# One M2 tile in 64-row halves between the score bursts of a quad, in an attention and MLP kernel on one core

## The chip, the cores and the metric

The kernel runs on one core of a Trainium2 chip. The time is the device time of one execution in microseconds (us); the figure given for a kernel is the median of its runs. A profiled execution gives, beside that, the span from its first to its last instruction. TensorE is called PE in the profile, its weight loads PEld, VectorE is DVE, ScalarE is ACT, GpSimd is POOL, SyncE is SP.

## What is computed

Causal attention with a decay made of a cumulative sum, for 8 batches of 8 heads, 576 positions and 64 values a head; then a two-layer MLP with SiLU over the 4608 tokens. The reference, cut to this:

```python
# q, k, v: (8, 8, 576, 64); f: (8, 8, 576); w_in: (512, 2048); w_out: (2048, 512), all float32
scores = q @ k.transpose(0, 1, 3, 2) / sqrt(64)
cum = cumsum(log(clip(f, 1e-4, 1.0)), axis=-1)
scores = where(causal, -1e9, scores + cum[..., :, None] - cum[..., None, :])
attn = softmax(scores, axis=-1)
x = (attn @ v).transpose(0, 2, 1, 3).reshape(4608, 512)
h = x @ w_in
out = (h * sigmoid(h)) @ w_out
```

## The kernel before

**Units and quads.** Two heads of one batch make a unit n (32 of them); two units, n and n+1, make a quad m = 0 to 15. The first 128 positions of every head are done ahead of the quads, in a first part of the kernel; each quad does the other 448 positions of its four heads.

**Attention of a unit.** scores(n, c) makes the transposed scores in three bursts c = 0, 1, 2 (L444 to L472). A head has 64 values, so its matmuls contract over 64 rows; the two heads of a unit lie in the two halves of the array's rows, and each pair of matmuls (i = 0, 1) writes to two PSUM banks. A burst takes one tile `sc` of two banks from the pool psc, which has two such tiles, and ScalarE reads it with exp into `u` (c = 0, 1 and part of 2) and `ut` (the last 64 positions, L467). mask(n) (L474) and mask_tail(n) (L480) set the entries above the diagonal to zero on VectorE. attend(n) (L490) multiplies with the values: 18 matmuls of 128x65 from `u` (L506) and 10 from `ut` (L515) into a tile `dn` of pbig, of which the fifth of each five on `ut` reads the part that mask_tail writes; then VectorE takes the reciprocal of the sums (L523) and divides (L524).

**Loads.** turn(n) casts unit n+2 on POOL and transposes it by a DMA on the SP queue (L427) into one of three tiles `qkT`; prepare(n) issues the loads of unit n+4 on SP and converts values on POOL; back(m) brings a quad's result into the MLP's layout, from quad 3 to 14 by two DMA transposes on SP (L538, L542; the list BY_DMA).

**The MLP.** The tokens form 13 groups of 512, 256 or 384 columns (GW): group 0 to 2 hold the first 128 positions, the others the rest of one batch each, or the last 64 positions of four batches. M1 makes a group's hidden layer in 16 chunks: m1_chunk(g, fc) runs four matmuls over all 128 rows into a tile `hp` of pbig (L567), ScalarE computes tanh of half of it (L575), VectorE makes the activation in `gt` (L576). `gt` has two buffers. M2 makes 128 tokens' output: m2_part(g, tb, part) runs 4 of the 16 matmuls of 128x512 (L612) into a tile `po` of pbig; after the fourth part ScalarE copies it with a factor 0.5 into `osb` (L622), and a DMA on the POOL queue stores it. `po` of one tile, `hp`, `dn` and other tiles share the four banks of pbig, in turn.

**The order.** Every engine's order is the program's. Attention and MLP are woven by hand: between the pieces of a quad stand slots, slot(us), that call fill(us). fill plans M1 chunks and M2 parts for as long as its budget is above zero, at fixed prices of 0.863 us an M2 part and 0.650 us an M1 chunk of 384 columns (0.437 for 256); what it overdraws is kept in at["left"] and comes off the next slot. wanted() chooses M1 or M2 so that M2 of the group before proceeds evenly with M1 of a group (L641 to L654). M1 of a group may not begin while M2 is more than one group behind. A slot then issues the stores that were recorded before it, and counts down the groups that wait to become ready.

Of the kernel before, what the change touches and what calls it, by code (L numbers as in the profile page):

```python
# [18 lines left out]
def kernel(  # L19
# [540 lines left out]
    def m1_chunk(g, fc):  # L560
        w = GW[g]
        if fc == 0:
            gts[g] = gpool.tile([P, NFC, w], BF16, name="gt", tag="gt")
        gt = gts[g]
        hp = pbig.tile([P, w], FP32, name="hp", tag="big")
        for cc in range(NCC):
            nc.tensor.matmul(  # L567
                hp[:, :],
                lhsT=w_in_bf[:, cc, fc * P : (fc + 1) * P],
                rhs=xcols(g, cc),  # L570
                start=(cc == 0),
                stop=(cc == NCC - 1),
            )
        th = tpool.tile([P, w], BF16, name="th", tag="th")
        nc.scalar.activation(out=th[:, :], in_=hp[:, :], func=ACT.Tanh, scale=0.5)  # L575
        nc.vector.scalar_tensor_tensor(  # L576
            out=gt[:, fc, :],
            in0=th[:, :],
            scalar=1.0,
            in1=hp[:, :],  # L580
            op0=ALU.add,
            op1=ALU.mult,
        )
# [4 lines left out]
    def store(n):  # L588
        n = max(n, 0)
        for q_, dst, src in stores[:n]:  # L590
            q_.dma_start(out=dst, in_=src)  # L591
        del stores[:n]
# [33 lines left out]
                stores.append((q_, out[t0 : t0 + r.stop - r.start, m0:m1], osb[r, :]))  # L626


    M1 = [(g, fc) for g in range(NG) for fc in range(NFC)]
    M2 = []  # L630
    for g in range(NG):
# [3 lines left out]
    at = {"m1": 0, "m2": 0, "left": 0.0}  # L635
    ready: set[int] = set()
    open2 = {"w": False}

    begin: dict[int, tuple[int, int]] = {}

    def wanted(a, c):  # L641


        g1 = M1[a][0] if a < len(M1) else NG
        g2 = M2[c][0] if c < len(M2) else NG
        can1 = g1 in ready and not (M1[a][1] == 0 and g1 > g2 + 1)
        can2 = open2["w"] and c < len(M2) and g2 < g1
        if not can1 or not can2:
            return 1 if can1 else 2 if can2 else 0
        a0, c0 = begin.get(g1, (M1[a][1], c)) if M1[a][1] else (0, c)  # L650
        c1 = sum(M2_OF[:g1])
        f1 = (M1[a][1] - a0 + 0.5) / (NFC - a0)
        f2 = (c - c0 + 0.5) / max(1, c1 - c0)
        return 1 if f1 <= f2 else 2  # L654

    def step(force=0):

        a, c = at["m1"], at["m2"]
        want = wanted(a, c)
        if not want:  # L660
            return None
        g1 = M1[a][0] if a < len(M1) else NG
        g2 = M2[c][0] if c < len(M2) else NG
        can1 = g1 in ready and not (M1[a][1] == 0 and g1 > g2 + 1)
        can2 = open2["w"] and c < len(M2) and g2 < g1
        kind = force if (force == 1 and can1) or (force == 2 and can2) else want
        if kind == 1:
            if M1[a][1] == 0:
                begin[g1] = (0, c)
            m1_chunk(g1, M1[a][1])  # L670
            at["m1"] += 1
            t = 4 * (GW[g1] / 2.4 + 2.5)
        else:
            m2_part(*M2[c])
            at["m2"] += 1
            t = 4 * (DM / 2.4 + 2.5)
        return t

    def behind():
        t = sum(4 * (GW[g] / 2.4 + 2.5) for g, _ in M1[at["m1"] :] if g in ready)  # L680
        t += sum(4 * (DM / 2.4 + 2.5) for g, _, _ in M2[at["m2"] :] if g in ready)
        return t / 1000
# [49 lines left out]
    scores0(0, bans[0])  # L732
    weights()
    setup_pool.__exit__(None, None, None)
    gpool = ctx.enter_context(tc.tile_pool(name="gpool", bufs=2))
    convert_v0(0)
    load_w_in(0)
    turn0(1, 0)
# [100 lines left out]
    def turn(n):  # L839
        if 0 < n < NU - 2:  # L840
            cast_qk(n + 2)
            transposes(n + 2)

    def prepare(n):
# [13 lines left out]
        if p >= 2:  # L858
            for c in range(2 * (p - 2), 2 * (p - 1)) if b > 0 else range(NM * (p - 2)):
                convert_v(b + 1, c)  # L860

    LAG = 13.0
    pending: list = []

    def slot(us_, *ends):
        n = len(stores)
        fill(us_, 0, ends)
        store(n)
        for x in pending:
            x[0] -= 1  # L870
        while pending and pending[0][0] == 0:
            ready.update(pending.pop(0)[1])

    for m in range(NQ):
        n = 2 * m
        piece = 1.7 if m < 2 else 2.4
        scores(n, 0)
        scores(n, 1)
        turn(n)
        if m > 0:  # L880
            back(m - 1)
            if m % 2 == 0:
                b = m // 2 - 1
                pending.append([2, [REST_OF[b]] + ([TAILS_OF[b][0]] if b == NM - 1 else [])])
        prepare(n)
        slot(piece, 1, 0)
        mask(n)
        scores(n, 2)
        scores(n + 1, 0)
        turn(n + 1)  # L890
        prepare(n + 1)
        slot(piece, 1, 0)
        mask_tail(n)
        mask(n + 1)
        scores(n + 1, 1)
        scores(n + 1, 2)
        mask_tail(n + 1)
        slot(piece, 1, 0)
        attend(n)
        attend(n + 1)  # L900
        slot(min(3.5, max(0.8, behind() - LAG)) if m > 1 else 0.8)
    back(NQ - 1)
    ready.update([REST_OF[B - 1], TAILS_OF[B - 1][0]])
    for x in pending:
# [35 lines left out]
```

## Time and profile before

| what | value | where from |
|---|---|---|
| time, median of 3 runs | 343.55 us | runs (343.11 to 345.07) |
| span of the profiled execution | 342.2 us | page |
| median less that span | 1.35 us | difference |
| M2 matmuls of 128x512 (L612) | 560 | groups by shape |
| score matmuls on 64 rows (L459) | 768 | groups by shape |
| evictions of 128x512 (L622) | 35, mean 609 ns | groups by shape |
| quad 7, first score to first score of quad 8 | 150.36 to 164.91 us | TensorE's timeline |

The profile is of one execution; its span lies a little under the times of the runs, which also hold what is ahead of the first and behind the last instruction. A matmul's duration in it is modelled, since matmuls are pipelined: two starts tell more than a duration. The 13 groups' M1 and M2 and the 16 quads fill the span to about 280 us; behind that stand only M1 and M2.

### The profile page before, as it was taken

Reading aid. Unit: us, or ns where it says so; the run is one execution under the profiler, and the core shown is the slowest. Engines: PE = TensorE matmul, PEld = TensorE weight load, DVE = VectorE, ACT = ScalarE, POOL = GpSimd, SP = SyncE. Lnnn points to the kernel's source line nnn. Section 1 sums busy time; section 2 is a strip of 40 time slices with the busy share of each in tenths; the row PEclk is TensorE's granted clock in tenths of the full one; section 3 lists DMA queues with packets and bytes.
Section 4 is the critical chain, followed back from the end, with each engine's and each line's share of the span. In section 5 each row is a group of like instructions: output and inputs, shape, how many; then the busy total and the mean of one; then the engine's idle time right before and its main releaser. Section 6 shows DMA issues by size and latency. Waiting matters only on the chain.

```text
span 342.2 us, 8881 instructions
## 1 busy us (share of the span) xinstructions
PE 334.3 (98%) x3560; PEld 198.6 (58%) x3560; DVE 180.5 (53%) x387; ACT 216.8 (63%) x401; POOL 130.0 (38%) x227
## 2 busy tenths in 40 slices
PE   7999999999999999999999999999999999999995
PEld 3645655567656556566465666656656565555654
DVE  4665736357647547357445563655746364444330
ACT  5857645877687676857759677595685944454431
POOL 8895317732618307327325422612830000001011
PEclk9999999999999999999999999999999999999999
DMA  8999999999699889999999789989994010001012
GB/s 154 185 184 221 192 192 155 233 207 190 142 172 205 188 177 168 180 210 156 174 188 188 171 156 202 169 170 165 165 186 101 22 42 33 31 32 61 33 53 72
DMA packets 142457, 50.67 MB, mean 148 GB/s; under 512 B 133328, under 2 KB 139728, under 8 KB 142416
## 3 DMA queue, kind: packets, MB, share of 16 engines
q1 hardware_dynamic: 132400, 32.93, 56.7%
q0 software_dynamic: 9856, 17.04, 21.5%
q8 instruction: 28, 0.46, 0.6%
q10 hardware_dynamic: 160, 0.13, 0.1%
q14 instruction: 13, 0.11, 0.1%
HBM read 36.85 MB, written 9.44 MB: 135 GB/s over the span
## 4 chain that ended last, share of the span: by engine, by line
PE 66%; DMA 14%; SPq 9%; POOL 6%; issue 3%; ACT 0%; POOLq 0%
PE po L612 29%; PE hp L567 25%; DMA vf<-in_v_dram 6%; PE sc L459 5%; SPq L158 5%; PE dn L506 4%; DMA w_out_bf<-in_moe_w_out_dram 3%; PE dn L515 2%; SPq L427 2%; DMA qkT<-qkb 2%; POOL qkb L399 1%; DMA qkb<-in_k_dram 1%; SPq L168 1%; SPq L179 1%; DMA qf<-in_q_dram 1%
## 5 line engine op out<-in xcount | busy, mean ns | idle before, releaser
L576 DVE SCALAR_TENSOR_TENSOR gt<-th,hp 128x384 bf16<-128x384 bf16 (+2 forms) x208 | 105.8, 522 | 119.0 <-ACT th L575 115.5
L575 ACT ACTIVATE th<-hp 128x384 bf16<-128x384 f32 (+2 forms) x208 | 95.2, 478 | 84.3 <-PE hp L567 82.0
L612 PE MATMUL po<-w_out_bf,gt 128*128 128x512 bf16 (+1 forms) x592 | 145.3, 374 | 0.0
L567 PE MATMUL hp<-x,w_in_bf 128*128 128x384 bf16 (+2 forms) x704 | 128.1, 321 | 0.2
L567 PEld LDWEIGHTS <-w_in_bf 128*128 128x128 bf16 x832 | 79.9, 98 | 56.5 <-issue 0.7
L463 ACT ACTIVATE u<-sc 128x1024 bf16<-128x1024 f32 (+1 forms) x96 | 75.3, 822 | 9.5 <-PE sc L459 9.5
L612 PEld LDWEIGHTS <-gt 128*128 128x128 bf16 x592 | 53.3, 98 | 47.9 <-issue 2.5
L591 POOL DMA_DIRECT2D out_dram<-osb x38 | 21.0, 552 | 93.7 <-ACT osb L622 66.7
L413 POOL TENSOR_TENSOR vp<-vf,w_bf 128x520 bf16<-128x520 f32 (+1 forms) x32 | 34.4, 1078 | 41.0 <-DMA vf<-in_v_dram 35.1
L622 ACT ACTIVATE osb<-po 128x512 f32<-128x512 f32 (+1 forms) x37 | 22.1, 597 | 18.9 <-PE po L612 18.9
L399 POOL CAST qkb<-qf 128x384 bf16<-128x384 f32 x32 | 16.7, 521 | 41.9 <-DMA qf<-in_q_dram 41.2
L459 PE MATMUL sc<-qkT 64*128 64x128 bf16 (+1 forms) x640 | 26.9, 207 | 0.9 <-DMA qkT<-qkb 0.8
L459 PEld LDWEIGHTS <-qkT 64*128 64x128 bf16 x640 | 18.4, 94 | 12.5 <-issue 10.2
L467 ACT ACTIVATE ut<-sc 128x640 bf16<-128x640 f32 x32 | 23.3, 729 | 0.0
L476 DVE TENSOR_TENSOR u<-u,tri 128x768 bf16<-128x768 bf16 x32 | 22.1, 690 | 1.2 <-ACT u L463 1.2
L399 POOL CAST qkb<-kf 128x384 bf16<-128x384 f32 x32 | 17.7, 554 | 13.0 <-DMA kf<-in_k_dram 12.8
L506 PEld LDWEIGHTS <-u 128*128 128x128 bf16 x576 | 20.8, 98 | 2.5
L506 PE MATMUL dn<-vp,u 128*128 128x65 bf16 x384 | 21.8, 194 | 0.0
L524 DVE TENSOR_TENSOR xr<-dn,rec 128x448 bf16<-128x448 f32 x32 | 20.0, 624 | 1.1
L506 PE MATMUL dn<-v,u 128*128 128x65 bf16 x192 | 19.8, 194 | 0.0
L482 DVE TENSOR_TENSOR ut<-ut,trit 128x128 bf16<-128x128 bf16 x32 | 11.2, 351 | 15.6 <-ACT ut L467 15.6
L567 PE MATMUL hp<-xt,w_in_bf 128*128 128x256 bf16 x128 | 17.7, 273 | 0.0
(68 smaller groups left out, 203.0 us busy)
## 6 DMA issues: line engine op xcount, KB each, us to landing
out_dram<-osb POOLq DMA_DIRECT2D x32, 256.0 KB, 3.3
vf<-in_v_dram SPq DMA_DIRECT2D x26, 256.0 KB, 4.7
qf<-in_q_dram SPq DMA_DIRECT2D x64, 96.0 KB, 2.9
kf<-in_k_dram SPq DMA_DIRECT2D x64, 96.0 KB, 3.1
w_in_bf<-in_moe_w_in_dram POOLq DMA_DIRECT2D x4, 512.0 KB, 6.9
w_out_bf<-in_moe_w_out_dram POOLq DMA_DIRECT2D x4, 512.0 KB, 9.6
vf<-in_v_dram POOLq DMA_DIRECT2D x6, 256.0 KB, 10.3
qkb<-in_q_dram POOLq DMA_DIRECT2D x8, 128.0 KB, 5.1
```

The costliest lines, as they stand in the source:

```text
L399: nc.gpsimd.tensor_copy(out=t2[:, c0 : c0 + NR, :].rearrange("p c x -> p (c x)"), in_=t[:, :, :, :].rearrange("p c h d -> p (c h d)"),)
L413: nc.gpsimd.tensor_tensor(out=vbf[b][r, c, :, :], in0=vst[b][c][r, :, :], in1=w_bf[r, c + 1, b * H : (b + 1) * H, None].to_broadcast([n, H ...
L459: nc.tensor.matmul(sc[:, i, o : o + q1 - q0], lhsT=kt, rhs=t[r, q0:q1], start=True, stop=True)
L463: nc.scalar.activation(out=u[:, :, c * SM : c * SM + w], in_=sc[:, :, 0:w], func=ACT.Exp, scale=scale)
L467: nc.scalar.activation(out=ut[:, :, 0:3:2, :].rearrange("p k i t -> p i k t"), in_=sc[:, :, T0 : T0 + (NM + 1) * ST].rearrange("p i (k t) ...
L476: nc.vector.tensor_tensor(out=x, in0=x, in1=tri[:, None, None, :].to_broadcast([P, 2, NR, P]), op=ALU.mult)
L506: nc.tensor.matmul(dn[:, i * NR + c - 1, :], lhsT=u[:, i, o : o + P], rhs=vals(kb, i), start=(kb == 0), stop=(kb == c),)
L567: nc.tensor.matmul(hp[:, :], lhsT=w_in_bf[:, cc, fc * P : (fc + 1) * P], rhs=xcols(g, cc), start=(cc == 0), stop=(cc == NCC - 1),)
L575: nc.scalar.activation(out=th[:, :], in_=hp[:, :], func=ACT.Tanh, scale=0.5)
L576: nc.vector.scalar_tensor_tensor(out=gt[:, fc, :], in0=th[:, :], scalar=1.0, in1=hp[:, :], op0=ALU.add, op1=ALU.mult,)
L612: nc.tensor.matmul(po[:, :], lhsT=gt[:, fc, tb * P : (tb + 1) * P], rhs=w_out_bf[:, fc, m0:m1], start=(fc == 0), stop=(fc == NFC - 1),)
L622: nc.scalar.activation(out=osb[:, :], in_=po[:, :], func=ACT.Copy, scale=0.5)
```

## The change

From m = 4 on, a quad asks whole() for an M2 tile whose group M1 has finished. whole() first runs the rest of a tile that is partly done, and charges those parts to the budget; if there is no whole tile of an earlier group, the quad runs as before. With a tile, the quad's order is another: the three slots between the bursts are gone. m2_rows(g, tb, half) stands between the first and second and between the second and third pair of bursts. It contracts 64 rows at a time: for each of 8 of the 16 fc, two matmuls, rows 0 to 63 into one tile of pbig and rows 64 to 127 into another. m2_join then adds the two tiles on VectorE in two operations, with the factor 0.5, into `osb`. After the bursts come attend(n), mask_tail(n+1), a slot of 1.3, attend(n+1), a slot of 2.4 and the last slot as before. The row tile itself is not charged to the budget.

The planner changes as well: M2 may be two groups behind from m = 2 on, and from m = 4 M2 runs in the slots only when more than 12 parts of groups ahead of M1's are left; behind the loop this is taken back. `gt` therefore has three buffers, in three tags; the first of them gives its memory to another pool after group 0.

```diff
@@ m1_chunk @@
-            gts[g] = gpool.tile([P, NFC, w], BF16, name="gt", tag="gt")
+            gts[g] = gpools[g % 3].tile([P, NFC, w], BF16, name="gt", tag=f"gt{g % 3}")
@@ after m2_part @@
+    def m2_rows(g, tb, half):
+        gt = gts[g]
+        if half == 0:
+            pos[g, tb] = [pbig.tile([P, DM], FP32, name="pr", tag="big") for _ in range(2)]
+        for fc in range(half * NFC // 2, (half + 1) * NFC // 2):
+            for z, po in enumerate(pos[g, tb]):
+                r = slice(z * D, (z + 1) * D)
+                nc.tensor.matmul(
+                    po[:, :],
+                    lhsT=gt[r, fc, tb * P : (tb + 1) * P],
+                    rhs=w_out_bf[r, fc, :],
+                    start=(fc == 0),
+                    stop=(fc == NFC - 1),
+                )
+
+    def m2_join(g, tb):
+        lo, hi = pos[g, tb]
+        store(len(stores) - 3)
+        osb = opool.tile([P, DM], FP32, name="osb", tag="osb")
+        nc.vector.tensor_scalar(
+            out=osb[:, :], in0=lo[:, :], scalar1=0.5, scalar2=None, op0=ALU.mult
+        )
+        nc.vector.scalar_tensor_tensor(
+            out=osb[:, :], in0=hi[:, :], scalar=0.5, in1=osb[:, :], op0=ALU.mult, op1=ALU.add
+        )
+        for r, b, s0 in rows_of(g, tb):
+            t0 = b * S + s0
+            stores.append((nc.gpsimd, out[t0 : t0 + r.stop - r.start, :], osb[r, :]))
@@ the planner @@
+    lag = {"g": 1, "parts": 0}
...
-        can1 = g1 in ready and not (M1[a][1] == 0 and g1 > g2 + 1)
+        can1 = g1 in ready and not (M1[a][1] == 0 and g1 > g2 + lag["g"])
         can2 = open2["w"] and c < len(M2) and g2 < g1
+        if can1 and can2 and lag["parts"]:
+            return 2 if sum(M2_OF[:g1]) - c > lag["parts"] else 1
@@ ahead of the quads @@
-    gpool = ctx.enter_context(tc.tile_pool(name="gpool", bufs=2))
+    gpool = ctx.enter_context(tc.tile_pool(name="gpool", bufs=1))
+    first_pool = tc.tile_pool(name="first", bufs=1)
+    gpools = [first_pool.__enter__(), gpool, gpool]
...
+    def whole():
+
+        while at["m2"] < len(M2) and M2[at["m2"]][2] and wanted(at["m1"], at["m2"]):
+            t = step(2)
+            at["left"] -= t / 1000
+        a, c = at["m1"], at["m2"]
+        if c >= len(M2) or M2[c][2]:
+            return None
+        g1 = M1[a][0] if a < len(M1) else NG
+        return M2[c][:2] if M2[c][0] < g1 else None
+
...
+    def passed():
+        for x in pending:
+            x[0] -= 1
+        while pending and pending[0][0] == 0:
+            ready.update(pending.pop(0)[1])
@@ the loop over the quads @@
+        if m == 2:
+            assert at["m2"] >= M2_OF[0]
+            first_pool.__exit__(None, None, None)
+            gpools[0] = ctx.enter_context(tc.tile_pool(name="third", bufs=1))
+            lag["g"] = 2
+        if m == 4:
+            lag["parts"] = 12
+        rows = whole() if m > 0 and BY_DMA[m - 1] else None
         scores(n, 0)
         scores(n, 1)
         turn(n)
...
         prepare(n)
+        if rows:
+            at["m2"] += 4
+            m2_rows(*rows, 0)
+            mask(n)
+            scores(n, 2)
+            scores(n + 1, 0)
+            turn(n + 1)
+            prepare(n + 1)
+            m2_rows(*rows, 1)
+            mask_tail(n)
+            mask(n + 1)
+            scores(n + 1, 1)
+            scores(n + 1, 2)
+            m2_join(*rows)
+            passed()
+            attend(n)
+            mask_tail(n + 1)
+            slot(1.3)
+            attend(n + 1)
+            slot(2.4)
+            slot(min(3.5, max(0.8, behind() - LAG)))
+            continue
         slot(piece, 1, 0)
...
+    lag["parts"] = 0
     back(NQ - 1)
```

More of the change, by code (lines that the diff above doesn't have):

```diff
@@ L663, in step @@
         g2 = M2[c][0] if c < len(M2) else NG
-        can1 = g1 in ready and not (M1[a][1] == 0 and g1 > g2 + 1)
+        can1 = g1 in ready and not (M1[a][1] == 0 and g1 > g2 + lag["g"])
         can2 = open2["w"] and c < len(M2) and g2 < g1
@@ L868, in slot @@
         store(n)
[L869 to L872, printed above, removed]
+        passed()
     for m in range(NQ):
@@ L885 @@
         prepare(n)
+        if rows:
[12 more added lines that the diff above has]
+            m2_join(*rows)
+            passed()
+            attend(n)
[5 more added lines that the diff above has]
+            continue
         slot(piece, 1, 0)
```

## The prediction

> **What bounds the kernel.** I read the page first, then TensorE's timeline over one quad in the middle (quad 7 of 0 to 15, 150.36 to 164.91 us), then those of ScalarE and VectorE beside it, then the groups by shape. All times are us unless marked ns.
>
> ```profile
> span 342.2 us, 8881 instructions
> PE 334.3 (98%) x3560; PEld 198.6 (58%) x3560; DVE 180.5 (53%) x387; ACT 216.8 (63%) x401; POOL 130.0 (38%) x227
> PEclk9999999999999999999999999999999999999999
> ```
>
> TensorE is busy 98% of the span at full clock; no other engine passes 63%. In quads 5 to 15 I compared each matmul's start with its predecessor's plus its streaming time: apart from one wait of 0.11, nothing but changes of the array's mode adds time. So what is taken off TensorE's stream comes off the end, and any new wait of TensorE is added in full.
>
> ```profile
> 149.77 0.65 PE L567 MATMUL hp<-x,w_in_bf 128*128 128x384 bf16 x3
> 150.36 0.40 PE L459 MATMUL sc<-qkT 64*128 64x128 bf16 x8
> 150.59 0.33 PE L459 MATMUL sc<-qkT,kT 64*128 64x384 bf16 x2
> 150.75 0.22 PE L459 MATMUL sc<-qkT 64*128 64x128 bf16 x2
> 150.91 1.04 PE L612 MATMUL po<-w_out_bf,gt 128*128 128x512 bf16 x4
> 151.78 2.11 PE L567 MATMUL hp<-x,w_in_bf 128*128 128x384 bf16 x12
> ```
>
> The first column is the start, the durations are modelled, so I use starts. M1 matmuls of 384 columns follow each other every 0.1625 (151.78 on). The last of the first three starts at 150.10 and the scores at 150.36 instead of 150.26: 0.10 to enter the 64-row mode. The last pair of scores, at 150.75, takes 0.056 like the four pairs before it (0.23 for eight matmuls); M2 could start at 150.81 and starts at 150.91: another 0.10 to leave. Over all switches of the trace the first step is 0.096 and 0.092 too long and the step after it 0.008 and 0.010: **0.206 for a round trip**. The pair of 64x384 ends 0.16 after it starts (150.59 to 150.75), which is one matmul's time: two 64-row halves in different rows of the array and different PSUM banks run together.
>
> **What the change takes off.** The planner's counters, followed through the new code by its own prices (0.863 for an M2 part, 0.650 for an M1 chunk of 384), put the row path into quads 5 to 15, 11 quads; in quad 4 M2 has no tile of an earlier group. Each had three round trips and keeps one: 22 x 0.206 = **-4.5**. The tile itself is 16 pairs of 64x512 for 16 matmuls of 128x512, which start every 0.216. From the 64x384 row a pair costs the same; were the halves serial, 11 x 16 x 0.216 = +38. I take the row, with up to 0.008 a pair (+1.4) for the range. The page "TensorE: Matmul & The Clock Gate" of the Trainium skill, section "Measured speedup vs the span model", reports 3.07 instead of 4 for four row tiles at 512 columns; by that share an estimate is 0.28 a pair and +11 in all, which the 64x384 pair speaks against.
>
> **What it adds: a wait of scores(n+1,0).** psc has two buffers, so scores(n+1,0) waits for the exp of scores(n,1). Two row halves of 8 x 0.216 = 1.73 now stand where slots of 2.4 stood.
>
> ```profile
> 150.85 1.94 ACT L463 ACTIVATE u<-sc 128x1024 bf16<-128x1024 f32 x2
> 251.07 0.60 ACT L622 ACTIVATE osb<-po 128x512 f32<-128x512 f32 x1 [0.37 <-PE po L612]
> 251.56 1.94 ACT L463 ACTIVATE u<-sc 128x1024 bf16<-128x1024 f32 x2
> 62.43 1.02 ACT L463 ACTIVATE u<-sc 128x1024 bf16<-128x1024 f32 x1
> 63.50 0.40 PE L459 MATMUL sc<-qkT 64*128 64x128 bf16 x8
> ```
>
> From a quad's first score on, the two exps end at 2.43 where an M1 chunk's tanh stands before them (150.36 to 152.79) and at 2.54 where an eviction does (quad 14, 250.96 to 253.50). Quad 0 shows this very wait: exp ends at 63.45, the scores start at 63.50, 0.05 later. TensorE now arrives at 0.45 + 1.73 + 0.21 (scores(n,2)) = 2.39: it waits 0.05 to 0.10 in six quads and 0.20 in the five (6, 8, 10, 13, 15) where whole() has just finished a tile whose eviction stands before the exps. Sum **+1.55**. Behind it on TensorE stand the second row half and the third burst, all of which move by the wait; ScalarE then gets exp(n+1,0) from 2.59 on but is busy with exp(n,2) until 3.43, so it loses nothing. The third burst does not wait: exp(n+1,0) ends at 4.47, its buffer is wanted at 4.77.
>
> **What it adds: a wait of attend(n+1).** M2 parts that whole() runs are charged to the budget, so slot(1.3) can come out empty. Quad 5 ends with a budget of -0.07 and one part of tile (3,2) done; whole() runs three (-2.66), and 1.3 more is still below zero. The same happens in quads 8, 10 and 13 (three, two and one part). There attend(n+1) follows attend(n) directly, and its matmuls on the tail need mask_tail(n+1), which on VectorE stands behind mask(n+1), the join and attend(n)'s division.
>
> ```profile
> L476 DVE TENSOR_TENSOR u<-u,tri 128x768 bf16<-128x768 bf16 x32 | 22.1, 690 | 1.2 <-ACT u L463 1.2
> L292 DVE CAST kT<-tp 128x512 bf16<-128x512 f32 x8 | 5.5, 689 | 4.5 <-PE tp L285 4.5
> L523 DVE RECIPROCAL rec<-dn 128x7 f32<-128x7 f32 x32 | 6.4, 199 | 2.2 <-PE dn L515 2.2
> L524 DVE TENSOR_TENSOR xr<-dn,rec 128x448 bf16<-128x448 f32 x32 | 20.0, 624 | 1.1
> L482 DVE TENSOR_TENSOR ut<-ut,trit 128x128 bf16<-128x128 bf16 x32 | 11.2, 351 | 15.6 <-ACT ut L467 15.6
> L236 DVE TENSOR_SCALAR f_sb<-f_sb 64x576 f32<-64x576 f32 x1 | 0.5, 452 | 0.0
> ```
>
> The join's two operations on 512 floats from PSUM are not in the trace. The cast from PSUM at 689 ns is nearest (same shape, same source); L236 at 452 (SBUF only) bounds it below, and above I add the 0.13 by which mask_tail's mean, 351, exceeds its undisturbed 0.22: 0.45 to 0.82, I take 0.69. From the quad's first score: mask(n+1) 4.50 to 5.19, first half 5.10 to 5.80 (an independent operation starts 0.08 before the last one ends: two L576 of 0.55 take 1.02), second half 5.84 to 6.53, reciprocal 6.44 to 6.64, division to 7.30, mask_tail to 7.57. TensorE is free at 5.91 and would end attend(n+1) at 6.75; the last six matmuls of 0.03 wait until 7.62 and end at 7.80: 1.05, or 0.79 with the masks at 0.55 and 0.22. I take 0.9, four times: **+3.6**. Behind it on TensorE stands slot(2.4), for which no other engine is waiting. With a join of 0.45 it is 0.4 each, with 0.82 it is 1.3. Where the slot holds two M1 chunks (1.30), attend(n+1) reaches the mask at 7.87 and waits for nothing. Quad 15 (one chunk) pays some 0.25, quad 11 (three chunks of 256, so dn(n+1) takes dn(n)'s buffer) some 0.15: **+0.4**.
>
> The page "TensorEngine Tiling (Array Packing)", section "PSUM Bottleneck", advises evicting with both ScalarE and VectorE when row tiles fill PSUM faster; the change puts both halves on VectorE. With one half on ScalarE, which stands idle there, by that rule the wait would be about 0.3 and the sum near -1.4.
>
> **What it moves, at no cost.** The eviction (L622, 0.61) leaves ScalarE in 11 tiles; ScalarE was off the path. The M1 chunks gather in the last slots: one every 0.65 on TensorE, 0.42 on ScalarE and 0.47 on VectorE, and from a chunk's first matmul to its buffer free is 2.0, under the 2.6 that four buffers give; with one buffer fewer (1.95) each chunk of a long row would wait 0.05. No DMA is added; stores stay on POOL, now behind both casts of the quad; the row tile's store waits there for the join (6.53), ahead of the next quad's casts, which stood behind an eviction at 8.3 in quad 8 before. scores(n+1,0) comes 0.3 to 1.2 earlier in its quad, so its DMA-transposed qkT is wanted earlier. SP issues nearly without a gap, and qkT(17) lands at 166.72 for 167.94, 1.2 ahead; most odd units have 2 to 2.8. Where the slack is least (quad 6, 0.5; quad 8, 1.2) whole()'s parts push the scores back by 2.6, so I price it at nothing. The looser M2 order costs nothing: same matmuls, and the code behind the loop ends with the same tile.
>
> **Sum.** -4.5 + 1.55 + 3.6 + 0.4 = **+1.0**. Against the profiled 342.2 the span becomes 343.2; the median of the runs lies 1.35 above that span, so 343.55 becomes **344.5**. The first measured digit that can be told from no change I put at 0.5%, 1.7.
>
> **Rivals.** (a) *The waits stay short*: the tail's masks are ready in time, say because VectorE evicts 512 floats at L236's rate or the four empty slots get work. For it: the waits are differences of chains several us long. Against it: the VectorE order is fixed by the program. It leaves -4.5 + 1.55 = -3.0: 340.6. (b) *VectorE becomes the bound of the row quads*, the slower side: the join is dearer than 0.82. From 0.25 later on at mask_tail(n+1) the five quads with two chunks wait as well. At 1.0 an operation the four pay 1.5, the five 0.4: -4.5 + 1.55 + 6.0 + 2.0 + 0.4 = +5.4: 349. For it: mask_tail's mean is 1.6 times its undisturbed time, so VectorE is disturbed there. Against it: 53% busy. (c) *qkT lands late*, because the SP queue does not follow: six quads at some 0.5 make +3 more, 347.5. (d) *The halves do not overlap*: 382; the 64x384 pair speaks against it.
>
> **How the numbers follow.** Forecast 0.62, its own range 341.4 (waits by the low join, -2.1) to 347.2 (high join, 0.20 at every second burst, slower pairs). (a) 0.17, (b) 0.12, (c) 0.07, (d) 0.02. Of the forecast's share 0.43 lies within 0.5%, 0.16 slower, 0.03 faster; of (a) 0.15 is faster and 0.02 within. That gives faster 0.18, same 0.45, slower 0.37. The range for 8 in 10 takes in most of (a) and (c): 340.5 to 347.8.
>
> **What will show it.** L459 and the new matmuls adjacent without the 0.1 steps, two pairs starting 0.216 apart (else d); scores(n+1,0) 0.05 behind the end of an exp; the join's operations near 0.69 (else a or b); gaps of about 0.9 inside L515 in quads 6, 8, 10, 13 and none in 5, 7, 9. The forecast is wrong if other quads show such gaps or TensorE waits for a DMA.

## The result, and the profile after

The changed kernel takes 346.37 us (median of 17 runs, 344.67 to 349.08); the kernel before takes 344.86 us beside it (17 runs, 343.11 to 346.17). The ratio is 1.0049, 95% interval 1.0027 to 1.0072: slower by about the half per cent that was named as the least that can be told from no change. The forecast of +1.0 us stands beside +1.5 us. The forecast's 344.5 us was counted from the three runs shown then, whose median, 343.55, lies 1.3 us below that of the 17.

The page of the changed kernel, its span, the busy time of TensorE and the granted clock:

```profile
span 347.2 us, 9257 instructions
PE 335.3 (97%) x3736; PEld 204.3 (59%) x3736; DVE 195.5 (56%) x409; ACT 217.8 (63%) x390; POOL 129.7 (37%) x227
PEclk9999999999999999999999999999999999999999
```

TensorE is at full clock as before, but it is no longer free of waits. This profiled execution took 349.0 us, nearly the longest of the 17, and its span is 5.0 us over that of before; a second profile of the same kernel (the first experiment) has a span of 343.6. Both are accounted for below. For that I took, for each two matmuls that follow each other, the time between their starts less the streaming time (0.2158 us for 512 columns, 0.1625 for 384). What is left is a change of the array's mode (0.1) or a wait.

TensorE's timeline in quad 6 of the changed kernel, from the last scores of the first two bursts to the end of attend(n+1) (start, us busy, operation, what it waited for in brackets where it was idle):

```profile
141.24 0.22 PE L459 MATMUL sc<-qkT 64*128 64x128 bf16 x2
141.29 1.89 PE L636 MATMUL pr<-w_out_bf,gt 64*128 64x512 bf16 x16
143.02 0.22 PE L459 MATMUL sc<-qkT 64*128 64x128 bf16 x2
...
143.11 0.72 PE L459 MATMUL sc<-qkT 64*128 64x64 bf16 x16
143.65 1.91 PE L636 MATMUL pr<-w_out_bf,gt 64*128 64x512 bf16 x16
...
146.89 0.20 PE L506 MATMUL dn<-v,u 128*128 128x65 bf16 x1
...
147.76 0.20 PE L515 MATMUL dn<-v,ut 128*128 128x65 bf16 x1
147.80 0.26 PE L515 MATMUL dn<-vp,ut 128*128 128x65 bf16 x3
148.33 0.20 PE L515 MATMUL dn<-vp,ut 128*128 128x65 bf16 x1 [0.28 <-DVE ut L482]
```

The last pair of scores starts at 141.24 and the first row pair at 141.29, one pair's streaming time later: the 0.1 step is gone. Sixteen row matmuls take 1.73 (141.29 to 143.02), the time of eight full ones. So the two things that the change is made of work. The price shows in two places. Scores of 64 columns that start at 143.11 last 0.72 in place of 0.50: inside that group scores(n+1,0) waits 0.20 for the exp before it. And inside attend(n+1), from 146.89 on, TensorE loses 0.86 by the starts (the bracket gives 0.28, since it counts from the modelled end of the matmul before). ScalarE's last exps of the quad, and VectorE's mask_tail(n+1):

```profile
145.81 1.30 ACT L463 ACTIVATE u<-sc 128x1024 bf16<-128x1024 f32 x2 [0.48 <-PE sc L459]
146.99 0.71 ACT L467 ACTIVATE ut<-sc 128x640 bf16<-128x640 f32 x1
```

```profile
148.00 0.28 DVE L482 TENSOR_TENSOR ut<-ut,trit 128x128 bf16<-128x128 bf16 x1
```

Three times the matmuls wait for one of these exps on ScalarE: 0.12 at 146.89, 0.05 at 147.16 and 0.25 at 147.76, each time starting 0.05 behind the end of one. The last six then wait another 0.44 for mask_tail(n+1), to 148.33. mask_tail, which stands behind the join and a division on VectorE, sets the end of it; by this timeline 0.42 of the 0.86 would be left without it, for ScalarE's exps.

The groups of VectorE by shape, for the join (L648, L651) and the mask in front of the wait:

```profile
L482 DVE TENSOR_TENSOR ut<-ut,trit 128x128 bf16<-128x128 bf16 x32 | 10.9, 340 | 22.6 <-ACT ut L467 22.6
L651 DVE SCALAR_TENSOR_TENSOR osb<-pr,osb 128x512 f32<-128x512 f32 x11 | 7.6, 692 | 1.1
L648 DVE TENSOR_SCALAR osb<-pr 128x512 f32<-128x512 f32 x11 | 7.5, 680 | 0.0
```

The join's operations take 680 and 692 ns where 690 was taken. All terms together, in us, changes against the profile of before:

| term | forecast | profile after | second profile of it |
|---|---|---|---|
| changes of mode in quads 5 to 15, 66 to 22, at 0.103 | -4.5 | -4.5 | -4.5 |
| scores(n+1,0) waits for an exp | +1.55 | +1.52 | +1.52 |
| attend(n+1) in quads 6, 8, 10, 13 | +3.6 | +4.21 | +3.75 |
| the same in quads 11 and 15 | +0.4 | +0.72 | +0.50 |
| the same in quads 5, 7, 9, 12, 14 | 0 | +2.13 | +0.36 |
| the wait that before has in quad 7 | 0 | -0.11 | -0.11 |
| TensorE waits in quads 0 to 4 (1.60 before) | 0 | +1.18 | -0.25 |
| sum | +1.0 | +5.1 | +1.3 |
| span less 342.24 | | +4.98 | +1.33 |

The sums meet the spans to 0.2, so nothing large is missing. Two rows make nearly all the difference between the two profiles of one kernel: the waits of the quads that were to wait for nothing, and those of quads 0 to 4, where no row tile stands yet. There the first profile waits 2.35 for qkT (1.16 in the kernel before), the second not at all for qkT, but 0.90 behind a mask_tail of 2.17. The largest wait of the other row, in the profile after (VectorE behind the bursts of quad 5, then GpSimd, then TensorE at the end of attend(n+1) of quad 5):

```profile
128.58 1.42 DVE L476 TENSOR_TENSOR u<-u,tri 128x768 bf16<-128x768 bf16 x1 [0.69 <-ACT u L463]
129.92 0.68 DVE L648 TENSOR_SCALAR osb<-pr 128x512 f32<-128x512 f32 x1
...
131.54 0.62 DVE L524 TENSOR_TENSOR xr<-dn,rec 128x448 bf16<-128x448 f32 x1
132.08 1.06 DVE L482 TENSOR_TENSOR ut<-ut,trit 128x128 bf16<-128x128 bf16 x1
```

```profile
128.53 2.38 POOL L413 TENSOR_TENSOR vp<-vf,w_bf 128x520 bf16<-128x520 f32 x2 [4.28 <-DMA vf<-in_v_dram]
...
132.01 1.05 POOL L413 TENSOR_TENSOR vp<-vf,w_bf 128x520 bf16<-128x520 f32 x1
```

```profile
132.02 0.26 PE L515 MATMUL dn<-vp,ut 128*128 128x65 bf16 x3
133.20 0.20 PE L515 MATMUL dn<-vp,ut 128*128 128x65 bf16 x1 [0.92 <-DVE ut L482]
```

mask(n+1) takes 1.42 in place of 0.56 and mask_tail(n+1) 1.06 in place of 0.22, each while GpSimd converts v (convert_v, L413). mask_tail starts 0.07 after the conversion and ends 0.08 after it. The operations between, which read PSUM (L648, L651, L523, L524), are as long as ever. Over the whole profile mask_tail's median is 0.225 clear of a conversion and 0.63 under one (8 of 32), the mask's 0.56 and 0.81 (6 of 32), while the join's two are 0.68 and 0.69 in both cases. The kernel before has the same stretching (0.224 and 0.87 for mask_tail, 7 under a conversion), but there attend(n+1) comes later, and quads 5 to 15 wait 0.11 in all.

The Trainium skill's page "SBUF — State Buffer", section "Who interferes with whom", says that a VectorE instruction with two inputs in SBUF contends with a GpSimd instruction that reads SBUF, and that whichever issues first keeps the other off for its whole length. The rows agree: the masks have two SBUF inputs, and 1.06 is the conversion's 1.05.

### The profile page after: what moved, and what is told of

It reads as the page before. It is cut to its first block, busy times and chain, and to the rows that moved or that the text cites. A ratio compares the mean times of both kernels' runs of the same rounds, so it can differ in the third digit from the quotient of the medians.

```text
span 347.2 us, 9257 instructions
## 1 busy us (share of the span) xinstructions
PE 335.3 (97%) x3736; PEld 204.3 (59%) x3736; DVE 195.5 (56%) x409; ACT 217.8 (63%) x390; POOL 129.7 (37%) x227
## 4 chain that ended last, share of the span: by engine, by line
PE 59%; SPq 17%; DMA 10%; issue 5%; ACT 4%; DVE 3%; POOL 2%; POOLq 0%; DVEq 0%
PE hp L567 23%; PE po L612 18%; SPq L158 7%; PE pr L636 5%; DMA qf<-in_q_dram 5%; SPq L427 4%; SPq L542 3%; PE sc L459 3%; DMA qkT<-qkb 3%; PE tp L285 2%; SPq L538 2%; PE wm L232 1%; PE dn L506 1%; ACT u L463 1%; PE dn L515 1%
## 5 line engine op out<-in xcount | busy, mean ns | idle before, releaser
L576 DVE SCALAR_TENSOR_TENSOR gt<-th,hp 128x384 bf16<-128x384 bf16 (+2 forms) x208 | 107.0, 522 | 73.1 <-ACT th L575 65.2
L567 PE MATMUL hp<-x,w_in_bf 128*128 128x384 bf16 (+2 forms) x704 | 122.8, 321 | 0.2
L612 PE MATMUL po<-w_out_bf,gt 128*128 128x512 bf16 (+1 forms) x416 | 96.8, 371 | 0.0
L612 PEld LDWEIGHTS <-gt 128*128 128x128 bf16 x416 | 39.3, 98 | 35.5 <-issue 0.2
L413 POOL TENSOR_TENSOR vp<-vf,w_bf 128x520 bf16<-128x520 f32 (+1 forms) x32 | 34.5, 1082 | 37.7 <-DMA vf<-in_v_dram 31.6
L636 PE MATMUL pr<-w_out_bf,gt 64*128 64x512 bf16 x352 | 41.8, 376 | 0.0
L476 DVE TENSOR_TENSOR u<-u,tri 128x768 bf16<-128x768 bf16 x32 | 20.4, 636 | 29.4 <-ACT u L463 29.3
L622 ACT ACTIVATE osb<-po 128x512 f32<-128x512 f32 (+1 forms) x26 | 15.2, 585 | 34.5 <-PE po L612 34.5
L459 PE MATMUL sc<-qkT 64*128 64x128 bf16 (+1 forms) x640 | 28.6, 206 | 2.2 <-DMA qkT<-qkb 1.6
L459 PEld LDWEIGHTS <-qkT 64*128 64x128 bf16 x640 | 20.0, 94 | 13.4 <-issue 6.0
L636 PEld LDWEIGHTS <-gt 64*128 64x128 bf16 x352 | 17.4, 94 | 15.3
L524 DVE TENSOR_TENSOR xr<-dn,rec 128x448 bf16<-128x448 f32 x32 | 20.0, 624 | 1.1
```

The source lines that it names most:

```text
L413: nc.gpsimd.tensor_tensor(out=vbf[b][r, c, :, :], in0=vst[b][c][r, :, :], in1=w_bf[r, c + 1, b * H : (b + 1) * H, None].to_broadcast([n, H ...
L459: nc.tensor.matmul(sc[:, i, o : o + q1 - q0], lhsT=kt, rhs=t[r, q0:q1], start=True, stop=True)
L567: nc.tensor.matmul(hp[:, :], lhsT=w_in_bf[:, cc, fc * P : (fc + 1) * P], rhs=xcols(g, cc), start=(cc == 0), stop=(cc == NCC - 1),)
L576: nc.vector.scalar_tensor_tensor(out=gt[:, fc, :], in0=th[:, :], scalar=1.0, in1=hp[:, :], op0=ALU.add, op1=ALU.mult,)
L612: nc.tensor.matmul(po[:, :], lhsT=gt[:, fc, tb * P : (tb + 1) * P], rhs=w_out_bf[:, fc, m0:m1], start=(fc == 0), stop=(fc == NFC - 1),)
L636: nc.tensor.matmul(po[:, :], lhsT=gt[r, fc, tb * P : (tb + 1) * P], rhs=w_out_bf[r, fc, :], start=(fc == 0), stop=(fc == NFC - 1),)
```

## The experiments

### The same kernel again

No edit.

> The changed kernel unaltered, for a second profile. Main theory (22 mode round trips saved, 4.5 us; given back by TensorE's waits for scores(n+1,0), 1.5 us, and for attend(n+1), 4 to 7 us): the steps of 0.09 and 0.20 at the second burst of all 11 row quads and the waits of about 0.86 us inside attend(n+1) of quads 6, 8 and 10 come again to 0.05; the larger waits of quads 5, 7, 11 and 13 (1.36, 0.77, 0.53, 1.64 us in the first profile) differ, since there a mask on VectorE runs beside a GpSimd multiplication whose start depends on a DMA. Rival (the loss is DMA, seen as TensorE waiting for qkT in quads 1 to 4): the waits before quad 5 differ from the 3.0 us of the first profile and carry the difference between runs. Time 345 to 349.

It measured 346.18 us (12 runs), ratio 1.0037 (1.0006 to 1.0068), and gave the last column of the table above. What repeats to a few hundredths are the changes of mode, the wait for the exp, and 0.80 to 0.86 in each of quads 6, 8 and 10. What does not repeat goes with the conversion of v: it waits for the load of vf (the bracket of the first GpSimd row above), so it meets the masks in one execution and misses them in another.

### The conversion of v left out

This kernel leaves out the conversion for batches 2 to 7, which then use the values of batches 0 and 1; TensorE's work is unchanged.

```diff
         vbf[b] = vps[b % 2]
+        if b > 1:
+            return
         r = slice(0, P) if c < NR else slice(ST, P)
```

> The changed kernel with GpSimd's multiplication of the values (convert_v) left out for batches 2 to 7, so that their attention uses the values of batches 0 and 1; everything else stays. Main theory: where this multiplication runs, a mask on VectorE (two operands from SBUF) takes 0.6 to 1.4 us in place of 0.22 or 0.55, and this makes the waits of quads 5, 7, 9, 11 and 13 that the profiles show beyond the ones at the second burst and those of the empty slots. Without it no mask after quad 4 lasts over 0.85 us, quads 5, 7 and 9 show nothing but the 0.09 at the second burst, quad 13 falls to about 1.0, and quads 6, 8 and 10 keep theirs; waits in quads 5 to 15 fall to about 5 us, from 6.1 and 8.6 in two profiles. Rival (VectorE's own work is the delay): the waits of the odd quads stay.

It measured 345.09 us, ratio 1.0024 (1.0001 to 1.0046). Quads 5, 7 and 9 keep 0.09 each, the wait for the exp alone; quad 13 loses 0.81 in attend(n+1), like quads 6, 8 and 10 (0.80 to 0.94), where it had lost 1.64 and 1.34. VectorE and then TensorE behind quad 5, for the same place as above:

```profile
128.31 0.56 DVE L478 TENSOR_TENSOR u<-u,tri 128x768 bf16<-128x768 bf16 x1 [0.67 <-ACT u L465]
128.79 0.68 DVE L650 TENSOR_SCALAR osb<-pr 128x512 f32<-128x512 f32 x1
...
130.96 0.21 DVE L484 TENSOR_TENSOR ut<-ut,trit 128x128 bf16<-128x128 bf16 x1
```

```profile
131.46 0.20 PE L517 MATMUL dn<-v,ut 128*128 128x65 bf16 x1
...
131.61 0.19 PE L517 MATMUL dn<-v,ut 128*128 128x65 bf16 x1
```

The masks take 0.56 and 0.21, and mask_tail is done at 131.17, ahead of the matmuls that read it. So it is the conversion that makes quads with two chunks in the slot of 1.3 wait, and the 0.8 of those where that slot is empty (6, 8, 10, 13) is there without it. The times alone do not tell this kernel from the changed one, since their intervals overlap; the traces do.

### Full rows in the same order

```diff
-            for z, po in enumerate(pos[g, tb]):
-                r = slice(z * D, (z + 1) * D)
-                nc.tensor.matmul(
-                    po[:, :],
-                    lhsT=gt[r, fc, tb * P : (tb + 1) * P],
-                    rhs=w_out_bf[r, fc, :],
...
+            nc.tensor.matmul(
+                pos[g, tb][fc % 2][:, :],
+                lhsT=gt[:, fc, tb * P : (tb + 1) * P],
+                rhs=w_out_bf[:, fc, :],
```

> The changed kernel with the row tile made by 16 matmuls of 128x512 over all rows, even fc into one of the two banks and odd fc into the other; banks, join and order stay. This puts the two removed mode round trips of each of the 11 quads back and nothing else. Main theory: 22 x 0.206 = 4.5 us more on TensorE's stream, of which 1.5 is taken from the waits at the second burst that TensorE now reaches 0.2 us later: 3.0 us over the changed kernel, 348.5 to 350. Rival (the saving was never there, pairs of halves cost more than a full matmul): no slower than the changed kernel.

It measured 348.78 us (6 runs), ratio 1.0115 (1.0076 to 1.0155), 2.6 us over the changed kernel on the same chip. TensorE at the start of its quad 5:

```profile
122.80 0.22 PE L459 MATMUL sc<-qkT 64*128 64x128 bf16 x2
122.95 1.90 PE L634 MATMUL pr<-w_out_bf,gt 128*128 128x512 bf16 x8
124.78 0.23 PE L459 MATMUL sc<-qkT 64*128 64x128 bf16 x2
```

The step from scores to M2 is 0.15 again where the row pair came after 0.05, and the one back is 0.10 too long as well. The trace has 66 changes of mode (+4.5) and no wait for the exp (-1.5), which makes 3.0; the saving is real, and it is the order around it that costs.

### The new order of M2 alone

```diff
-        rows = whole() if m > 0 and BY_DMA[m - 1] else None
+        rows = None
```

> The changed kernel without the row path: three gt buffers, M2 up to two groups behind and the rule of 12 parts stay, every quad runs its three slots. Main theory: the new order of M1 and M2 costs and saves nothing; the same time as the kernel before, within 0.3%, 33 mode round trips in quads 5 to 15 and under 0.5 us of waits there. Rival (the looser order or the third buffer costs something): 1 us or more over the kernel before.

It measured 346.59 us (7 runs), ratio 1.0069 (1.0041 to 1.0097): slower than before by about 2.4 us without any row tile. Quads 5 to 15 wait 2.87 where before waits 0.11, half of it in quad 10, whose timeline of TensorE has:

```profile
197.57 1.47 PE L567 MATMUL hp<-xt,w_in_bf 128*128 128x256 bf16 x12
199.44 0.60 PE L567 MATMUL hp<-xt,w_in_bf 128*128 128x256 bf16 x4 [0.39 <-DVE gt L576]
```

and ScalarE's beside it:

```profile
197.62 1.04 ACT L463 ACTIVATE u<-sc 128x1024 bf16<-128x1024 f32 x1
198.52 0.97 ACT L575 ACTIVATE th<-hp 128x256 bf16<-128x256 f32 x3
200.07 0.39 ACT L575 ACTIVATE th<-hp 128x256 bf16<-128x256 f32 x1 [0.59 <-DVE gt L576]
```

With M2 held back, M1 chunks of 256 columns stand four in a row, each 0.43 on TensorE, while ScalarE still works at the burst's exps: the first tanh starts at 198.52, and the fourth chunk waits until VectorE, behind that tanh, has emptied the bank that it takes (by the starts 0.56, and 0.40 in the next such run). In the same slots of the kernel before one M2 part of 0.86 and one or two chunks alternate. The same matmuls in another order are not free: this was the forecast's clearest mistake of reasoning. In the changed kernel the cost is smaller, since much of the M1 and M2 work sits elsewhere: of its waits only 0.1 us, in quad 11, is inside such a run.

### Both attends later

```diff
-            attend(n)
-            mask_tail(n + 1)
             slot(1.3)
-            attend(n + 1)
+            mask_tail(n + 1)
             slot(2.4)
+            attend(n)
+            attend(n + 1)
```

> Both attends of a row quad stand behind the slots of 1.3 and 2.4, and mask_tail(n+1) between these slots; the planner's sequence is the same chunk for chunk. Main theory: the waits inside attend(n+1) (7.1 us in the profile of the changed kernel, 4.0 by the prediction) fall to under 1 us in all, those at the second burst stay at 1.5; time 3 to 6 us under the changed kernel, that is 340.5 to 343 where the kernel before has 344 to 345. Rival (VectorE itself is the bound of the row quads): TensorE waits as long, now for hp's buffers, and the time stays within 1 us of the changed kernel. Rival (DMA): the same.

It measured 346.37 us, ratio 1.0034 (1.0004 to 1.0064): no gain over the changed kernel. The waits for mask_tail are gone, but M1 chunks now stand directly behind the bursts, and their tanh stands on ScalarE behind the last exps: in quad 7 the first tanh starts at 159.11, 1.67 after the first chunk, VectorE stands idle 0.70 for it, and the fifth chunk waits 0.21 for the bank that the first one holds until 160.22. The same 0.21 comes in six of the eleven row quads; in quad 11 chunks wait 0.83, most of it for the join; in quads 5, 10 and 13 TensorE waits 0.47, 0.69 and 0.43 at an attend. Quads 5 to 15 wait 5.5 in all, against 6.1 and 8.6. A further 1.8 in quad 4 and 1.1 in quad 1 are waits for qkT. So two chains end late behind the bursts, the exps on ScalarE and the join and divisions on VectorE, and moving one consumer handed the wait to the next.

### Nine pairs, then seven

The kernel above, and in m2_rows:

```diff
-        for fc in range(half * NFC // 2, (half + 1) * NFC // 2):
+        for fc in ((range(0, 9), range(9, NFC))[half]):
```

> attend_late with the row tile divided into 9 and 7 pairs in place of 8 and 8, so that TensorE reaches scores(n+1,0) 0.22 us later, behind the end of the exp at 2.43 to 2.54 us. Main theory: the waits at the second burst (1.5 us in all) vanish and none comes at the third (buffer free at about 4.5 us, wanted at 4.56): 1.0 to 1.5 us under attend_late, 4 to 5 us under the kernel before. Rival: ScalarE is the bound of the burst section, and the wait moves to the third burst: no difference from attend_late.

It measured 345.6 us, ratio 1.0011 (0.9986 to 1.0036). scores(n+1,0) no longer waits, but the third burst waits 0.195 in all eleven quads, 2.1 us instead of 1.5: what the first half of the tile gained, the second is too short to cover. Between two bursts ScalarE's exps take longer than half a tile, so the split only chooses where TensorE waits.

### The charge put off

whole()'s parts are charged to the budget behind slot(1.3), so that no such slot is empty.

```diff
+        owed = at["left"]
         rows = whole() if m > 0 and BY_DMA[m - 1] else None
+        owed = owed - at["left"] if rows else 0.0
+        at["left"] += owed
...
             slot(1.3)
+            at["left"] -= owed
             attend(n + 1)
```

> The changed kernel with the parts that whole() ran charged behind the slot of 1.3 instead of before it, so that this slot always holds work; by the planner's counters 10 row quads are left (quad 8 runs as before). Main theory: the waits of 0.9 us inside attend(n+1) in quads 6, 8 and 10 vanish, that of quad 13 (one chunk) shrinks by half or more; waits in quads 5 to 15 fall to 2 to 4.5 us, of which 1.5 at the second bursts; time 1.5 to 3 us under the changed kernel. Rival (other work of VectorE is late next): the same waits at hp's buffers, and no gain.

It measured 345.0 us, ratio 1.0012 (0.9989 to 1.0035). Quads 6 and 10 keep 0.2 where they had 1.0; quad 8 no longer finds a tile and runs the old way. That the empty slots made these waits is thereby shown. Quads 7 and 9 show the conversion of v in this profile (1.0 and 1.35), so that quads 5 to 15 still wait 5.4.

### Half the columns at a time

The charge put off as above, the two slots changed about, and the tile made in two halves of 256 columns instead of two halves of fc: each half is joined as soon as it is done, the first between the bursts.

```diff
-        for fc in range(half * NFC // 2, (half + 1) * NFC // 2):
-            for z, po in enumerate(pos[g, tb]):
+        c = slice(half * DM // 2, (half + 1) * DM // 2)
+        pos[g, tb, half] = [pbig.tile([P, DM // 2], FP32, name="pr", tag="big") for _ in range(2)]
+        for fc in range(NFC):
+            for z, po in enumerate(pos[g, tb, half]):
...
-                    rhs=w_out_bf[r, fc, :],
+                    rhs=w_out_bf[r, fc, c],
...
+            m2_join(*rows, 0)
             m2_rows(*rows, 1)
...
-            slot(1.3)
-            attend(n + 1)
             slot(2.4)
+            at["left"] -= owed
+            attend(n + 1)
+            slot(1.3)
```

> owed with the slots of 2.4 and 1.3 exchanged, and the row tile made in two halves of 256 columns, each over all 16 fc, in place of two halves of fc: the first 256 columns are joined while the second are made, so that only two operations on 256 columns stand on VectorE between the third burst and attend(n)'s division. Main theory: 20 round trips saved, 4.1 us; the waits at the second burst stay at 1.5; those inside attend(n+1) go to under 0.3 in all, since mask_tail(n+1) is then ready at about 7.1 us after the quad's first score, or 8.0 beside GpSimd, and is wanted at 9.2. Span 2 us under that of the kernel before with equal waits before quad 5; time 342 to 343.5 where the kernel before has 344.9. Rival (pairs of 256 columns cost more than half of pairs of 512, since each has its own weight loads): over 0.109 us a pair, and the gain is lost.

It measured 346.02 us, ratio 1.0051 (1.0018 to 1.0085). Here no attend of quads 5 to 15 waits at all: what is left is 0.07 or 0.18 a quad for the exp, 0.65 in quad 11, and one new wait, in quad 8, which finds no tile here either:

```profile
166.07 0.28 PE L459 MATMUL sc<-qkT 64*128 64x64 bf16 x8
169.19 0.40 PE L459 MATMUL sc<-qkT 64*128 64x128 bf16 x8 [2.83 <-DMA qkT<-qkb]
```

By the starts it is 2.99 us. Without it this span, 343.0, would be 340.0. TensorE arrives at the second unit of quad 8 before that unit's qkT has landed. The issue of that transpose on SP, in the kernel before and in this one:

```profile
162.04 2.45 SPq L427 DMA_TRANSPOSE qkT<-qkb  x1
```

```profile
163.91 2.21 SPq L427 DMA_TRANSPOSE qkT<-qkb  x1
```

Before, qkT(17) landed at 166.72 and was wanted at 167.94. Here it is wanted at 166.20, 1.74 sooner, and lands at 169.14, 2.42 later. This is the forecast's rival (c), with a second cause beside its own: SP falls behind, and TensorE, freed of its other waits, comes sooner. Why SP issues it 1.87 later is not shown.

### Attention paced slower

```diff
-    LAG = 13.0
+    LAG = 10.0
```

> columns with LAG = 10.0 in place of 13.0: the last slot of a quad takes more M1 and M2 work, so attention runs later against SP's queue, and qkT(17) is wanted later. Theory: the wait for qkT in quad 8 falls from 2.99 to below 1, span 340.5 to 342, ratio 0.994 to 0.998. Rival: the work taken into the quads is missing at the end of the loop or the wait for qkT only moves to another quad: span 342.5 to 344, ratio 1.000 to 1.005.

It measured 345.06 us, ratio 1.0003 (0.9975 to 1.0031). The wait of quad 8 is gone, but with the other plan attends wait 1.87 and 1.73 in quads 7 and 9, which find no tile, behind mask_tails of 1.84 (quad 7), 1.35 and 1.07 (quad 9) beside GpSimd's work, and quad 14 waits 0.89 for qkT. Nothing is decided by it beyond that a slower pace alone does not help.

### The loads of v on GpSimd's queue

In the kernel with half columns, and for a control in the kernel before, which has no row tile:

```diff
-        nc.sync.dma_start(
+        nc.gpsimd.dma_start(
             out=t[r, :, 0:D],
```

> columns with the four loads of v of a batch (load_v) issued by GpSimd's DMA queue instead of SP's. Theory: what columns saved on the array's modes came back as 2.99 us of TensorE waiting for qkT(17) in quad 8, since SP issues without a gap and its four v loads of a batch (0.49 + 0.58 + 0.86 + 2.86 = 4.8 us at 151.9 to 156.9) stand ahead of the two transposes that quad 8 needs. Without them qkT lands some 4 us earlier in every second quad: the 2.99 goes, the waits of quads 5 to 15 come to 1.5 to 2.5, those of quads 0 to 4 stay at 0.5 to 1.5; the span is 339 to 341, 2 to 3 us below the kernel before, ratio 0.991 to 0.995. Rival: GpSimd issues them late (its casts and stores stand ahead, and the conversion of v waits for them), so the cast of q and k and with it qkT is as late as before: a span of 343 or more, and the wait for qkT in quad 8 or elsewhere stays above 1.

> The kernel before with the same move of load_v to GpSimd's queue, and nothing else: the control. Theory: the kernel before waits 1.60 in quads 0 to 4 (part of it for qkT) and 0.11 in quads 5 to 15, so a freer SP queue can give it at most 1.2, a ratio of 0.997 to 1.000. Rival: if it gains as much as columns does, then the row tile has no share in the gain; if it loses, GpSimd's queue is the worse place for these loads.

They measured 352.31 and 352.04 us, ratios 1.018 (1.0131 to 1.0228) and 1.016 (1.0107 to 1.0213). The half-column kernel loses it in quads 0 to 4: TensorE waits 13.6 us there, of which 8.1 are two waits for qkT and most of the rest is a lower clock behind them. The control loses as much, so this has nothing to do with the row tile.

In quads 5 to 15 the half-column kernel waits only 1.26 so, and the wait of quad 8 is gone. That suggested one more run, in which the loads of v move only from batch 4 on:

```diff
+        q_ = nc.gpsimd if b >= 4 else nc.sync
-        nc.sync.dma_start(
+        q_.dma_start(
```

> columns with the loads of v issued by GpSimd's queue only from batch 4 on (those issued from quad 6 on), SP's before. columns_vpool, with all of them there, waited 13.6 us in quads 0 to 4 and 1.26 in quads 5 to 15, where columns waited 1.32 and 4.90. Theory: the 2.99 us for qkT(17) in quad 8 goes, as it did there, and quads 0 to 4 stay as in columns, since their loads stay: waits of 1.3 to 1.6 and 1.3 to 2.0, span 342.24 - 20 round trips x 0.206 + 1.2 to 1.9 - 0.2 = 339.0 to 339.8, ratio 0.990 to 0.994. Rival: TensorE, 3 us earlier from quad 8 on, finds other qkT late (units 19, 25 and 29 had 2.3, 1.1 and 0.2 of slack in columns), since GpSimd's loads take the same DMA engines: span 341.5 to 344, ratio 0.998 to 1.004.

It measured 346.82 us, ratio 1.0055 (1.0026 to 1.0084): the rival. Quad 8 does not wait, but quads 7, 9 and 11 do, 3.26, 1.38 and 1.21 us, all for qkT. The DMA issues of the same 12 us (141 to 153 of each span) in the half-column kernel and in this one; the last number is the median time from issue to landing:

```profile
qf<-in_q_dram SPq DMA_DIRECT2D x4, 96.0 KB, 3.2
kf<-in_k_dram SPq DMA_DIRECT2D x4, 96.0 KB, 2.8
...
qkT<-qkb SPq DMA_TRANSPOSE x2, 3.7
```

```profile
qf<-in_q_dram SPq DMA_DIRECT2D x2, 96.0 KB, 6.1
kf<-in_k_dram SPq DMA_DIRECT2D x2, 96.0 KB, 8.2
...
qkT<-qkb SPq DMA_TRANSPOSE x1, 9.4
```

GpSimd issues its four loads beside SP's, and everything in flight takes longer: q 6.1 for 3.2, k 8.2 for 2.8, and the transpose 9.4 for 3.7, since its issue stands on SP for 5.95 (1.28 in the half-column kernel). So SP's queue alone was not what was short. The stretch from 112 to 170 us by windows, in the kernel before and in the half-column kernel (length, busy time of PE, PEld, DVE, ACT and POOL, clock, DMA's busy share, GB/s):

```profile
112.00:170.00 58.00, 58.00 (x657) 33.33 (x651) 31.25 (x68) 40.19 (x73) 23.09 (x40) 1.00 0.97 179
```

```profile
112.00:170.00 58.00, 55.13 (x783) 38.39 (x782) 35.33 (x79) 39.98 (x70) 21.59 (x37) 1.00 0.96 169
```

The DMA engines' busy share is 97% in this stretch of the kernel before, and 99% in that from 58 to 112 us. The share adds up what the packets took and passes 1 in other windows (1.18 further down), so it shows a crowded stage, not how much more could be moved. TensorE is the bound there, but with little to spare: what it gains in quads 5 to 9 these runs with half columns lose to waits for qkT. The Trainium skill's page "DMA: Bandwidth & Descriptors", section "Issuing engines are not separate DMA queues", says that transfers started from several engines run on the same 16 DMA engines, and that a further queue saves only issue time; the landing times above agree.

No kernel of these beat the one before: the nearest are at 1.0003, 1.0011 and 1.0012, each with an interval that holds 1.

## Why the prediction came out as it did

The direction and the size were right, and the two largest terms of it mainly for the reason that it gives. That +1.5 stands so near to +1.0 is in part luck: the three rows of the table that were put at nothing came to 3.2 together in one profile and to 0.0 in the other. The steps in turn:

- **What the change takes off, -4.5.** Confirmed, in the trace (66 changes of mode become 22) and by the run with full rows: 2.6 us slower, where 4.5 less the 1.5 of the exps is 3.0.
- **The row pair costs what a full matmul costs.** 16 row matmuls of 512 columns take 1.73; rival (d) is out.
- **The wait of scores(n+1,0), +1.55.** Measured 1.52: 0.09 where an M1 chunk stands before, 0.05 in quad 11, 0.20 behind an eviction. That the third burst does not wait holds too, and the run with nine pairs shows how little was left there.
- **The empty slots, +3.6.** The four quads are the right ones. 6, 8 and 10 cost 0.80 to 0.86 each where 0.9 was taken. Only quad 13 is larger (1.34 and 1.64), by the conversion of v; without it 0.81. The path was only half seen: the forecast has TensorE wait once, for mask_tail, but in quad 6 the first 0.42 of the 0.86 are waits for ScalarE's exps. So ScalarE does not "stand idle there" for half of the join either: it runs exps from 145.81 to 147.70, and the join runs from 145.83 to 147.31. The -1.4 that was estimated from that was not tested.
- **"Two-chunk quads (5,7,9,12,14) wait for nothing."** This step failed, and by the forecast's own sign (gaps in 6, 8, 10 and 13, none in 5, 7 and 9): in the first profile L515 has gaps of 1.08 and 0.77 in quads 5 and 7. The chain had the masks at their means, 0.69 and 0.35, which end mask_tail at 7.57, 0.30 before it is wanted at 7.87. But mask_tail's mean of 1.6 times the undisturbed time was not a little on each of 32: in the kernel before six of them took 0.45 to 1.12. The forecast named it as a hint for rival (b), "VectorE is disturbed there", and spread it; the price that belonged there is up to 0.9 more for a mask or a mask_tail that meets conversions. In the two profiles of the changed kernel this made 2.13 and 0.36, and some 0.5 to 0.8 more in quad 13. Rival (b) itself did not come about, since the join is not dear.
- **"The looser M2 order costs nothing."** This failed by itself: +2.4 us in the run without row tiles, from runs of chunks that four buffers cannot carry. The forecast had worked out the margin for chunks of 384 columns (2.0 against 2.6) and not for those of 256, which come every 0.43. In the changed kernel it shows as little more than the surplus of quad 11 (0.72 and 0.50 for the 0.4 of quads 11 and 15).
- **qkT at nothing.** Right for quads 5 to 15 of the changed kernel. In quads 0 to 4 its first profile waits 1.2 us more for qkT than the kernel before, its second 1.2 less. The forecast's 1.2 us of slack at qkT(17) was the place to watch: the version that took the other waits away met a wait of 2.99 there.

So the expected gain of 4.5 was made and given back within the same quads: 1.5 to the exps, 3.7 to the chains of VectorE and ScalarE behind the bursts (six quads), which leaves +0.7, and 0.9 to 3.2 more to GpSimd's interference, by the execution. What stays open: how much of the spread between executions of the changed kernel comes from the conversion of v and how much from waits for qkT in quads 0 to 4. The two rows differ by 1.8 and 1.4 us between the profiles, but no run separates them over many executions. Nor was a version tried that lightens the transfers themselves.

## What to carry to other kernels

Packing like work together to save an engine's changes of mode also takes away the filler that stood between its bursts, and the filler was hiding other engines' chains; price these chains from the burst's first instruction before counting the saving. A mean that is well above the undisturbed time of an instruction can be a few very long ones, here six of 32: find which, and put their full length into the chain that would wait. And before a bound is lifted, see how busy the next resource is in the same stage: here the DMA engines' share was 97 to 99%, and of the transposes from quad 5 on, those with the least room landed 0.5 and 1.2 us before they were wanted.

## What the runs showed of the hardware

- A VectorE operation on two SBUF inputs that starts just behind a GpSimd operation can last until that one ends: mask_tail's 0.22 becomes 1.06 beside a conversion of 1.05, the mask's 0.56 becomes 1.42 beside two of them, and in the second profile one mask_tail takes 2.17 beside three casts and a conversion. Operations with an input in PSUM keep their time (0.62, 0.68 and 0.69 beside a conversion and clear of one).
- Two 64-row matmuls of 512 columns in the two halves of the array run fully beside each other: pairs start 0.216 apart, the second half 0.002 to 0.020 after the first.
- A long TensorE wait can cost more than itself. In the half-column kernel with all loads of v on GpSimd's queue TensorE waited 4.8 us for qkT(1), up to 67.55. The windows behind it (columns as above) have the granted clock at half until about 73.5, which costs another 2.6 us. A wait of 3.34 in the same run, up to 110.48, was followed by 0.51 from 111 to 113; waits of 2.99 and 3.26 us in two other runs with half columns were followed by 1.00.

```profile
66.00:69.00 3.00, 1.45 (x11) 0.71 (x12) 0.00 (x0) 0.80 (x1) 2.15 (x3) 0.61 1.18 149
69.00:71.00 2.00, 2.00 (x9) 1.14 (x8) 0.00 (x0) 0.35 (x2) 1.96 (x4) 0.50 0.90 229
...
73.00:77.00 4.00, 4.00 (x70) 2.94 (x69) 1.78 (x5) 1.55 (x4) 2.65 (x5) 0.94 1.07 240
```
